# Signs of the first twelve weight pieces taken by ScalarE and multiplied in by GpSimd

## The chip, the cores and the metric

The kernel runs on one core of one Trainium2 chip. Time is device microseconds (us) for one execution. The engines are TensorE (PE; its weight loads are shown as PEld), VectorE (DVE), ScalarE (ACT), GpSimd (POOL) and SyncE (SP, which issues most of the DMAs). Each engine works through its own instructions in the order in which they stand; where it needs another engine's result it waits for a semaphore.

## The reference

A recurrent attention block (batch 4, 8 heads, 768 steps, head width 40) feeds a feed-forward block (3072 tokens, width 320, hidden width 2048):

```python
for t in range(S):
    y[:, :, t] = np.einsum('bhd,bhde->bhe', rt, state)
    Sa = np.einsum('bhde,bhe->bhd', state, at)
    state_decay = state * wt[:, :, None, :] - np.einsum('bhd,bhe->bhde', Sa, bt)
    state = state_decay + np.einsum('bhd,bhe->bhde', vt, kt)
...
h = x @ w_in
g = h * np.cos(h)
return (g @ w_out).astype(np.float32)
```

The two weight matrices `w_in` and `w_out` are given as 64-bit floats; everything else is 32-bit.

## The kernel before

**Recurrence.** The 768 steps are cut into 24 chunks of 32. Four chunks at a time share one stage that inverts small triangular matrices on VectorE, as a chain of short multiply and subtract pairs (L681 and L686 for the first four chunks, followed by the transposes L695 and L663). Each chunk then goes through short TensorE steps, named in the plan by letters: `t` (transposes of the state), `q`, `x`, `s` and `z`, with copies on ScalarE and VectorE between them (L811, L825, L850, L851, L869, the masks L875). After `z`, VectorE adds the new state and the output (L916, L925), and GpSimd multiplies both (L917 four times, L933 once, of 128x512). SyncE stores the output to a scratch tensor and reads it back, turned, as `xT`.

**Feed-forward.** Two chunks form a group of 256 tokens. For each of 12 groups TensorE multiplies `xT` by `w_in` (tile `ph`), ScalarE and VectorE form the product with the cosine, and TensorE multiplies this by `w_out` (tile `po`).

**Weights.** TensorE needs the weights as 32-bit floats, and the kernel turns the 64-bit values into these by hand, in 20 pieces of 128x512. The function is `rounded`; a piece goes through five steps, each a token in the plan with the piece's number:

- `wf`, `fetch`: SyncE loads the raw words, two 32-bit words for each value (L423).
- `wt`, `taken`: VectorE takes the mantissa's upper part (L431) and the exponent (L432) from the high word; ScalarE turns the exponent into the bits of a 32-bit power of two (Relu, L435).
- `wm`, `mantissa`: VectorE adds the low word (L444), ScalarE scales (L447).
- `wg`, `signed`: VectorE merges the high word's sign bit into the power of two (L438).
- `wp`, `product`: VectorE multiplies mantissa and signed power of two into the weight tile (L450).

The raw words lie in tiles that other stages use too (`gT` twice; `nt`, `u` and `inv` once each), the mantissa and the exponent in two buffers each. A new load into a tile waits until the last step that reads its old words is done.

**Order.** The order of all steps is written out in one string, `PLAN`; the token's place there is its place on each engine's queue that it uses. `K` and `B` tokens are filler matmuls on TensorE (tiles `busy` and `spare`), which compute nothing that is used. The pieces are worked on in the order 1, 2, 3, 0, 4, 6, 7, 9, 8, 10, 5, 11 and then 13, 12, 14 to 19. GpSimd also issues a few loads itself (L262 on POOL) and prepares operands: the copies L735, the product L741 and the copy L742, for which TensorE's transposes of `v`, `r` and `k` wait.

Of the kernel before, what the change touches and what calls it, by code (L numbers as in the profile page):

```python
# [9 lines left out]
F32 = mybir.dt.float32  # L10
I32 = mybir.dt.int32
U32 = mybir.dt.uint32
ALU = mybir.AluOpType
ACTF = mybir.ActivationFunctionType
# [114 lines left out]
def kernel(  # L129
# [43 lines left out]
    nc = tc.nc  # L173
# [55 lines left out]
    for n, fill in (("w", 1.0), ("a", 0.0), ("b", 0.0)):  # L229
        for i in range(4):  # L230
            x = slice((i - 2) * H * DP, (i - 1) * H * DP)
            if i < 2:
                t = const.tile([P, H, D if n == "b" else DP], F32, tag=f"nat_{n}{i}", name=f"nat_{n}{i}")
            else:
                t = {
                    "w": w_in_sb[:, 0, late:], "a": w_in_sb[:, 1, late:], "b": late_out
                }[n][:, x].rearrange("p (h d) -> p h d", h=H)
# [5 lines left out]
    for n in "kvr":  # L243
        t = const.tile([P, H, D], F32, tag=f"nat_{n}", name=f"nat_{n}")
# [163 lines left out]
    tick = constant(6).bitcast(BF16)[:, :1]  # L408

    WID = 512  # L410
    first_done, second_done = [], []

    def rounded(m, dst, src, by, by_sb):

        pool, tag = {"g": (sb2, "gT"), "n": (sb1, "nt"), "u": (sb1, "u"), "i": (sb1, "inv")}[WORDS[m]]
        t = {}

        def fetch():  # L420
            t["words"] = pool.tile([P, WID, 2], I32, tag=tag, name="words")
            for rows, cols, part in src:
                nc.sync.dma_start(  # L423
                    t["words"][rows, cols].rearrange("p n w -> p (n w)"), part.bitcast(I32)
                )

        def taken():
            hi = t["words"][:, :, 1]
            t["mant"] = sb2.tile([P, WID], I32, tag="mant", name="mant")
            t["expo"] = sb2.tile([P, WID], I32, tag="expo", name="expo")  # L430
            nc.vector.tensor_scalar(t["mant"], hi, 0xFFFFF, None, ALU.bitwise_and)  # L431
            nc.vector.tensor_scalar(  # L432
                t["expo"], hi, 20, 0x7FF, ALU.logical_shift_right, ALU.bitwise_and
            )
            nc.scalar.activation(t["expo"], t["expo"], ACTF.Relu, bias=to_bits, scale=2.0**23)  # L435

        def signed():
            nc.vector.scalar_tensor_tensor(  # L438
                t["expo"], t["words"][:, :, 1], -(2**31), t["expo"], ALU.bitwise_and, ALU.bitwise_or
            )  # L440

        def mantissa():
            frac = t["mant"].bitcast(F32)
            nc.vector.scalar_tensor_tensor(  # L444
                frac, t["words"][:, :, 0].bitcast(U32), 2.0**-32, t["mant"], ALU.mult, ALU.add
            )
            nc.scalar.activation(frac, frac, ACTF.Identity, bias=by_sb, scale=2.0**-20 * by)  # L447

        def product():
            nc.vector.tensor_tensor(  # L450
                dst, t["mant"].bitcast(F32), t["expo"].bitcast(F32), ALU.mult
            )

        return fetch, taken, mantissa, product, signed

    def weights():
# [5 lines left out]
        def put(dst, src, by, by_sb):  # L462
            if wide:
                work.append(rounded(len(work), dst, src, by, by_sb))
                return

            def fetch():
                for rows, cols, part in src:
                    nc.sync.dma_start(dst[rows, cols], part)

            none = lambda: None
            work.append((fetch, none, none, lambda: nc.scalar.mul(dst, dst, by), none))

        flat_out = w_out_sb.rearrange("p f n -> p (f n)")
        for j in range(NF // 4):
            cs = slice(j * WID, (j + 1) * WID)
            for i in range(2):
                put(
                    w_in_sb[:, i, cs], [(every, slice(0, WID), moe_w_in[i * P : (i + 1) * P, cs])],
                    0.5 / math.pi, by_in,  # L480
# [14 lines left out]
            first_done.append(len(work))  # L495
            for o in range(0, NF * DM, WID):
                if not 4 * j * DM <= o < 4 * (j + 1) * DM:
# [733 lines left out]
```

## Time and profile before

| What | Value |
|---|---|
| three runs, median (lowest to highest) | 762.61 us (758.38 to 766.61) |
| profiled execution | 755.39 us |
| its span, first to last instruction | 753.7 us |
| mean granted TensorE clock | 0.983 |
| busy share of PE, DVE, ACT, POOL | 93%, 71%, 53%, 33% |

The profile shows one execution. A row of the timeline gives start and duration in us, the engine, the source line, the operation, the tile that it writes and those that it reads, and how many instructions were put together; in brackets stands how long the engine had been idle and who ended that. A mean duration in a group of instructions is in ns. The chain of waits follows the work that ended last back from the end, and names at each step what released it.

The page's slices, each of 18.8 us, show the stages: until about 97 us VectorE is busy to eight or nine tenths and TensorE works on the recurrence of the first chunks; from then on TensorE is full.

```profile
PE   4659899999999999989999999999999999999995
DVE  7799888976467777568987758998367984534442
ACT  1335575775656665655645746546456444544442
POOL 8545304221241442450440442332242412321211
```

### The profile page before, as it was taken

Reading aid. Unit: us, or ns where it says so; the run is one execution under the profiler, and the core shown is the slowest. Engines: PE = TensorE matmul, PEld = TensorE weight load, DVE = VectorE, ACT = ScalarE, POOL = GpSimd, SP = SyncE. Lnnn points to the kernel's source line nnn. Section 1 sums busy time; section 2 is a strip of 40 time slices with the busy share of each in tenths; the row PEclk is TensorE's granted clock in tenths of the full one; section 3 lists DMA queues with packets and bytes.
Section 4 is the critical chain, followed back from the end, with each engine's and each line's share of the span. In section 5 each row is a group of like instructions: output and inputs, shape, how many; then the busy total and the mean of one; then the engine's idle time right before and its main releaser. Section 6 shows DMA issues by size and latency. Waiting matters only on the chain.

```text
span 753.7 us, 40220 instructions
## 1 busy us (share of the span) xinstructions
PE 702.8 (93%) x17956; PEld 578.2 (77%) x17956; DVE 534.8 (71%) x1199; ACT 398.0 (53%) x764; POOL 245.8 (33%) x427
## 2 busy tenths in 40 slices
PE   4659899999999999989999999999999999999995
PEld 2546577777777777878888888888888788888885
DVE  7799888976467777568987758998367984534442
ACT  1335575775656665655645746546456444544442
POOL 8545304221241442450440442332242412321211
PEclk9779999999999999999999999999999999999998
DMA  7667455564565657655656667557543212110000
GB/s 118 130 168 183 149 152 136 116 132 75 117 119 113 123 107 145 130 130 115 139 118 110 128 130 155 107 118 120 102 78 76 62 41 59 48 29 13 21 18 17
DMA packets 267580, 78.11 MB, mean 104 GB/s; under 512 B 229104, under 2 KB 260848, under 8 KB 267408
## 3 DMA queue, kind: packets, MB, share of 16 engines
q1 hardware_dynamic: 264976, 73.66, 46.7%
q8 instruction: 141, 2.31, 1.3%
q0 software_dynamic: 1344, 1.72, 1.2%
q10 hardware_dynamic: 1088, 0.16, 0.1%
q14 instruction: 31, 0.25, 0.1%
HBM read 54.53 MB, written 20.97 MB: 100 GB/s over the span
## 4 chain that ended last, share of the span: by engine, by line
PE 69%; DVE 13%; ACT 5%; DMA 4%; SPq 4%; issue 3%; POOL 1%; DVEq 0%; POOLq 0%; ACTq 0%
PE ph L210 28%; PE po L210 17%; PE dps L210 4%; PE x0ps L210 4%; PE gram L210 3%; PE p L210 3%; SPq L262 2%; PE sps L210 2%; PE qps L210 2%; DVE inv L659 2%; PE nps L210 2%; DVE inv_tmp L655 2%; DVE gT L1010 2%; PE sT L807 1%; DMA nat_v<-in_v_dram 1%
## 5 line engine op out<-in xcount | busy, mean ns | idle before, releaser
L210 PE MATMUL ph<-xT,w_in_sb 128*128 128x256 f32 x768 | 184.3, 386 | 2.5 <-issue 1.0
L210 PEld LDWEIGHTS ph<-xT,w_in_sb 128*128 128x128 f32 x768 | 139.8, 190 | 31.1 <-issue 12.0
L210 PE MATMUL po<-w_out_sb,gT 128*128 128x160 f32 (+1 forms) x624 | 130.3, 347 | 3.0 <-DVE gT L1010 2.3
L1002 DVE SCALAR_TENSOR_TENSOR turns<-turns,ph 128x512 f32<-128x512 f32 x96 | 63.6, 685 | 93.5 <-ACT turns L1000 93.2
L1000 ACT ACTIVATE turns<-ph,few 128x512 f32<-128x512 f32 x96 | 63.6, 686 | 120.2 <-PE ph L210 110.1
L210 PEld LDWEIGHTS po<-w_out_sb,gT 128*128 128x128 f32 x624 | 97.1, 190 | 21.5 <-DVE gT L1010 3.3
L917 POOL TENSOR_TENSOR qz<-qz,wc 128x160 f32<-128x160 f32 x92 | 40.0, 457 | 132.5 <-DVE qz L916 132.5
L1010 DVE TENSOR_TENSOR gT<-ph,turns 128x512 f32<-128x512 f32 x96 | 64.4, 684 | 21.1 <-ACT turns L1007 20.8
L1007 ACT ACTIVATE turns<-turns,few 128x512 f32<-128x512 f32 x96 | 69.3, 722 | 3.1
L1006 ACT ACTIVATE turns<-turns 128x512 f32<-128x512 f32 x96 | 60.1, 626 | 12.4 <-DVE turns L1002 12.3
L1090 POOL TENSOR_TENSOR s<-gT 128x256 f32<-128x256 f32 x36 | 26.9, 747 | 97.3 <-DVE gT L1086 97.3
L210 PE MATMUL ph<-xT,w_in_tail 64*128 64x256 f32 (+1 forms) x464 | 54.5, 396 | 0.0
L291 ACT COPY nat_a<-ws 128x416 f32<-128x416 f32 (+1 forms) x45 | 45.1, 1019 | 16.9 <-DMA wdv<-nat_a 5.7
L210 PE MATMUL po<-TW,gT 128*128 128x160 f32 x288 | 51.4, 300 | 1.8 <-DVE gT L1086 1.2
L659 DVE TENSOR_TENSOR inv<-inv,inv_tmp 128x31 f32<-128x31 f32 (+15 forms) x124 | 50.0, 404 | 4.2
L1082 POOL TENSOR_TENSOR s<-gT 128x256 f32<-128x256 f32 x36 | 27.2, 757 | 78.7 <-DVE gT L1010 72.7
L825 ACT COPY qz<-qps 40x256 f32<-40x256 f32 x92 | 33.8, 367 | 30.8 <-PE qps L210 29.3
L655 DVE TENSOR_TENSOR inv_tmp<-u,inv 128x31 f32<-128x31 f32 (+15 forms) x124 | 46.5, 375 | 2.7
L566 POOL TENSOR_TENSOR bn<-nat_b,rw 128x320 f32<-128x320 f32 x22 | 19.3, 878 | 84.8 <-DVE rw L565 39.2
L210 PEld LDWEIGHTS po<-TW,gT 128*128 128x128 f32 x288 | 42.9, 190 | 2.8 <-DVE gT L1086 1.9
L565 DVE RECIPROCAL rw<-nat_w 128x320 f32<-128x320 f32 x20 | 42.6, 2139 | 0.0
L916 DVE TENSOR_TENSOR qz<-dps,qz 128x160 f32<-128x160 f32 x92 | 29.2, 317 | 16.8 <-PE dps L210 16.8
(158 smaller groups left out, 1248.5 us busy)
## 6 DMA issues: line engine op xcount, KB each, us to landing
words<-in_moe_w_in_dram SPq DMA_DIRECT2D x8, 512.0 KB
xd<-yt SPq DMA_DIRECT2D x48, 80.0 KB
out_dram<-ot SPq DMA_DIRECT2D x24, 160.0 KB
nat_v<-in_v_dram SPq DMA_DIRECT2D x90, 40.0 KB
nat_k<-in_k_dram SPq DMA_DIRECT2D x90, 40.0 KB
nat_b<-in_b_dram SPq DMA_DIRECT2D x84, 40.0 KB
wd<-ws SPq DMA_DIRECT2D x5, 640.0 KB
nat_w<-wd SPq DMA_DIRECT2D x80, 40.0 KB
```

Of the source, the lines that this page charges most:

```text
L210: nc.tensor.matmul(o, lhsT=lhsT, rhs=rhs, start=start, stop=stop, skip_group_check=True)
L291: nc.scalar.copy(quad_part(n, q, i).rearrange("p (d t) -> p d t", t=C), ws[:, :, PARTS[i]].rearrange("p t d -> p d t"))
L565: nc.vector.reciprocal(rw, wn)
L655: nc.vector.tensor_tensor(tmp, u[:, j : j + 1, :j].to_broadcast([P, C - j, j]), x[:, j:, j : j + 1].to_broadcast([P, C - j, j]), ALU.mult,)
L659: nc.vector.tensor_tensor(x[:, j:, :j], x[:, j:, :j], tmp, ALU.subtract)
L825: nc.scalar.copy(pick(qz[rows], f * (NZ - C), (NZ, 2 * B), (1, C)), ps[f][rows, : 2 * B * C].rearrange("p (i t) -> p i t", t=C),)
L917: nc.gpsimd.tensor_tensor(z, z, wc.rearrange("p (b f m) -> p f m b" if re_laid("w", c // 4) else "p (f m b) -> p f m b", f=2, m=2)[:, :, : ...
L1000: nc.scalar.activation(t, u, ACTF.Identity, bias=rnd, scale=1.0)
L1002: nc.vector.scalar_tensor_tensor(t, t, -ROUND, u, ALU.add, ALU.subtract)
L1006: nc.scalar.activation(t, t, ACTF.Abs)
L1007: nc.scalar.activation(t, t, ACTF.Sin, bias=half_pi, scale=-2.0 * math.pi)
L1010: nc.vector.tensor_tensor(gT[:, 2 * e : 2 * e + 2, :n], phs[e], ns[e].rearrange("p (f t) -> p f t", f=2), ALU.mult)
```

## The change

For pieces 0 to 11 the step `wg` no longer runs on VectorE. Behind the Relu of `wt`, ScalarE takes the sign of the high word (seen as a 32-bit integer) and writes it back as +1.0 or -1.0 in place of the word; the step `wg`, at its old place in the plan, is a multiply of the power of two by this sign on GpSimd. Pieces 12 to 19 keep the merge on VectorE. The plan is the same.

```diff
     WID = 512
+    SIGNS = 12
...
             nc.scalar.activation(t["expo"], t["expo"], ACTF.Relu, bias=to_bits, scale=2.0**23)
+            if m < SIGNS:
+                nc.scalar.activation(hi.bitcast(F32), hi, ACTF.Sign)

         def signed():
+            if m < SIGNS:
+                power = t["expo"].bitcast(F32)
+                nc.gpsimd.tensor_tensor(power, power, t["words"][:, :, 1].bitcast(F32), ALU.mult)
+                return
             nc.vector.scalar_tensor_tensor(
                 t["expo"], t["words"][:, :, 1], -(2**31), t["expo"], ALU.bitwise_and, ALU.bitwise_or
             )
```

On GpSimd the new multiplies stand, in this order, between the loads and operands of the first three chunks: 1 and 2 before the copies L735 of chunk 2, 3 before the sums L917 and L933 of chunk 0, 0 between L933 and L741, 4, 6, 7, 9 and 8 among the following loads, 10 and 5 after the sums of chunk 1 and before the copies L735, 11 between these and the next L741.

## The prediction

> **What bounds the kernel now.** I read the page's slices first, then busy time by windows, the chain of waits in order of time, and the timeline of the stretch that the change touches. The windows (window in us, its length, then busy us and instructions of PE, PEld, DVE, ACT, POOL, then granted clock, DMA share and GB/s):
>
> ```profile
> 50.00:100.00 50.00, 43.17 (x1440) 30.70 (x1441) 45.82 (x97) 26.06 (x52) 18.04 (x26) 0.90 0.60 164
> ```
> ```profile
> 110.00:130.00 20.00, 19.30 (x429) 15.50 (x426) 16.74 (x33) 11.49 (x21) 8.36 (x16) 1.00 0.59 140
> 130.00:160.00 30.00, 28.35 (x828) 22.70 (x827) 26.62 (x53) 21.23 (x41) 9.18 (x18) 1.00 0.55 124
> ```
>
> From about 97 us on TensorE is full and its order is fixed, so whatever start it gets is carried to the end. Between 50 and 100 us the order is set by VectorE (45.8 of 50 us busy; much of the PE time there is filler), and this is where all twelve pieces are converted. The naive reading is therefore a gain: VectorE is full and the change takes twelve instructions from it. The first fence below is their group in that stretch; the chain of waits (start, us, what) says more:
>
> ```profile
> L438 DVE SCALAR_TENSOR_TENSOR expo<-words,expo 128x512 int32<-128x512 int32 x12 | 9.7, 818 | 0.2 <-ACT expo L435 0.2
> ```
> ```profile
> 67.42 0.72 ACT expo L435
> ...
> 68.83 0.51 ACT expo L435
> 69.46 1.33 ACT mant L447 x2
> ...
> 72.85 0.73 ACT expo L435
> 73.60 0.69 DVE expo L438
> ```
>
> The chain runs piece by piece through VectorE, ScalarE and back. L438 stands in it four times (52.47, 59.61, 73.60, 86.93) with 0.53+0.62+0.69+0.89 = 2.7 us. That, not 9.7, is the most that taking it away could give by this chain.
>
> **What is removed.** Twelve merges L438. One alone is 0.69 us, and 0.60 from its start to the next (80.58 to 81.18); the mean of 818 ns comes from those beside GpSimd.
>
> **What is added.** Twelve Signs on ScalarE, each right behind a Relu L435, in place on the high words (every second element, int32). No row shows one. Below lies the plain copy of 128x512 (0.59), above the re-ordering copy L291 (1.02 for 416 columns, so 1.25 for 512). I take the Relu's 0.72, the same type and size, which pushes what follows on ScalarE by 0.63 (68.83 to 69.46). Twelve multiplies of 128x512 on GpSimd. Nearest is L933, same size and engine, 1.26 to 1.72. One input fewer is L742's copy: 0.45 for 320, so 0.72 for 512, the lower end. Both inputs here lie in SBUF and one steps by two. I take 1.27, for this reason:
>
> ```profile
> 62.54 0.97 DVE L450 TENSOR_TENSOR w_out_sb<-mant,expo 128x512 f32<-128x512 f32 x1
> ...
> 62.93 1.72 POOL L933 TENSOR_TENSOR yt<-yt,wb 128x512 f32<-128x512 f32 x1
> 63.44 1.75 DVE L438 SCALAR_TENSOR_TENSOR expo<-words,expo 128x512 int32<-128x512 int32 x1
> ...
> 64.61 1.31 POOL L741 TENSOR_TENSOR kn<-nat_k,rw 128x320 f32<-128x320 f32 x1
> ...
> 65.29 1.17 DVE L450 TENSOR_TENSOR w_in_sb<-mant,expo 128x512 f32<-128x512 f32 x1
> 65.86 0.90 POOL L742 COPY vvm<-nat_v 128x320 f32<-128x320 f32 x1
> ```
> ```profile
> 117.39 1.26 POOL L933 TENSOR_TENSOR yt<-yt,wb 128x512 f32<-128x512 f32 x1
> ```
>
> Alone L933 takes 1.26 and L438 0.69. Together they take 1.72 and 1.75, and each ends about one lone duration after the other did: 63.51 + 1.2 = 64.7, + 0.6 = 65.2, + 0.8 = 65.9, + 0.6 = 66.5. They take turns. So a multiply costs VectorE its 1.27 us wherever VectorE has two-input SBUF work of its own, and this work replaces 0.60 us.
>
> The Trainium skill says the same as a rule (SBUF — State Buffer, "SBUF: two separate sides"): VectorE and GpSimd share one pair of ports under an exclusive lock, held for the whole instruction. These rows agree. By that rule the sum is the one below; without it, it is the first rival's.
>
> **The wait it adds.** The product L450 on VectorE now waits for the multiply, and the multiply for Sign and for its place on GpSimd's queue. From the end of Relu to the product: Sign 0.63, hand-over 0.08 (VectorE to GpSimd at 61.15 to 61.23), multiply 1.27, hand-over 0.03, in all 2.0 us. Before, these rows left (Relu's end to product, by piece): 1: 16.0, 2: 0.8, 3: 4.1, 0: 5.5, 6: 1.3, 4: 3.3, 7: 1.0, 9: 2.7, 8: 10.4, 10: 9.0, 11: 1.1, 5: 5.2. Four are under 2.0. Behind a waiting product stand on VectorE the next piece's two extractions, the copies L851 and masks L875 and L789 for which TensorE's recurrence waits, and the running sums L916.
>
> ```profile
> 72.85 0.72 ACT L435 ACTIVATE expo<-expo,few 128x512 int32<-128x512 int32 x1
> ...
> 73.51 0.72 ACT L447 ACTIVATE mant<-mant,few 128x512 f32<-128x512 f32 x1
> 73.60 0.69 DVE L438 SCALAR_TENSOR_TENSOR expo<-words,expo 128x512 int32<-128x512 int32 x1 [0.19 <-ACT expo L435]
> ...
> 74.58 0.68 DVE L450 TENSOR_TENSOR w_in_sb<-mant,expo 128x512 f32<-128x512 f32 x1
> ```
>
> **The sum, in the order of time.** Each step is the delay of the recurrence against before.
>
> 1. Up to 61 us, piece 1. On GpSimd its multiply stands behind four load issues (43.96 to 46.3), so it runs at 46.3 to 47.6, inside the chained inversion on VectorE (46.1 to 48.8, no idle, two SBUF inputs). It holds that up by its 1.27, about 1.2, up to the transpose L663 for which TensorE waits (52.61). The saved merge at 52.32 lies behind that. Piece 2's longer way makes the mask L875 late by 1.8, ending at 58.85; TensorE wants it at 59.95 and is itself 1.2 late: hidden. **+1.2.**
> 2. 61 to 66.4, pieces 3 and 0. GpSimd's order is multiply 3, the sums L917, L933, multiply 0, L741, L742. Multiply 3 lies before the sums and before the product L450 at 62.54, both free. Multiply 0 takes the turn that merge 0 had: 1.27 for 0.60. **+0.7.**
> 3. To 70.8, pieces 4 and 6. The chain is ScalarE: Relu, copies, Relu, then L447 twice, product 6 at 70.82. Two Signs come in (+1.26) and multiply 6 then needs 1.27: Relu 6 ends 69.57 + 1.26 + 0.08 + 1.27 + 0.03 = 72.2. **+1.4.**
> 4. Piece 7, the fence above: 73.57 + 2.0 = 75.6 for 74.58. **+1.0.**
> 5. Pieces 9 and 8. Two Signs push the copy L869 from 77.27 to 78.5; multiply 8 (78.7 to 80.0) then holds L444, which starts near 80.0 instead of 77.8; L447 ends 81.35, product 9 at 81.4 for 79.36. The two saved merges lie behind. **+2.0.**
> 6. 85 to 97, pieces 10, 5, 11. GpSimd's queue is in order: multiplies 10 and 5 stand ahead of the copies L735, multiply 11 ahead of L741. L741 ended at 91.4 and its transpose ran at 95.53. Now multiply 5 waits for Relu and Sign 5 (to 92.1, done 93.4), the copies end 94.3, multiply 11 95.6, L741 96.4. **+1.0.**
>
> Sum +7.3 us. From piece 12 on the code is as before, TensorE is the bound, and I see nothing that takes the delay back. On SyncE's queue, fetches now wait for the multiply instead of the merge, with loads of w, stores of yt and the read of xT behind them. The fetch at 55.61 is used at 66.39, so its 2 us are covered; the others move with the steps above.
>
> The profiled execution: 753.7 span + 1.7 around it = 755.4 us; with the sum, 762.7. The three runs have a median of 762.6, 7.2 above the profiled one, so I put the same sum on that: 769.9, say **770**.
>
> **Rivals.**
> *Multiplies beside VectorE.* If they did not take turns, step 1 goes, step 2 goes to 0, step 5 falls to the two Signs (1.3), step 6 to 0.3: +4.0, 766.6. Against it: the rows at 62 to 66. For it: none, except that VectorE's own work has gaps. 0.11.
> *The cover holds, not slower.* Eight of twelve products leave more than 2.0 us. If the ones under it are also hidden by other waits (VectorE already waits 0.61 and 1.56 us for TensorE before L916), the chain loses what L438 has in it: 0 to −2.7, so 760 to 762.6. It decides once multiplies end before the product's place in the queue at pieces 2, 6, 7, 11. Against it: at 6 and 7 the chain of waits goes right through this loop. 0.12.
> *Heavier multiplies.* At the 1.72 of the contended row, or with a price for the stepping input, some eight multiplies in the steps cost 0.45 more: +10.9, 773.5. A lower granted clock would add too: it is 0.50 where TensorE idles, at 50 to 58 us. 0.17.
> *Not what it says.* Sign might need its own function table. The trace has one ACT_TABLE_LOAD, 1.28 us; 24 of them would give +31 (793). The changed program has one as well. 0.01. The Trainium skill (ScalarE: Activation LUTs, "What ACT_TABLE_LOAD costs") has about 2.66 us a switch, the drain included, by which it would be an estimated +64 us.
>
> **Chances and range.** Forecast 0.59. One per cent is 7.6 us, about what a measurement of this kernel can tell from no change, and the sum lies almost on it. What is not in the sum (hand-overs, clock) only adds, so a little over half of the forecast (0.33) goes beyond, with the heavier case and the table: slower 0.51. Within: 0.26 of the forecast, 0.11, and most of the cover (0.08): 0.45. Faster by over 1% asks for more than the chain holds: 0.04. Range: from the edge of the cover (763) to the heavier case (773.5), with half the spread of the three runs (4) and a Sign at its upper end in the four chain steps (4 x 0.5) on top: 780.
>
> **What would show it.** Right: L438's successors on GpSimd near 1.3 to 1.7 us; products L450 waiting for GpSimd at pieces 6, 7, 9; inversion rows near 46 us stretched by about 1.2; the first real ph matmul at 104 instead of 96.8, and the rest shifted by as much. Wrong: that matmul before 99, products that do not wait, multiplies and VectorE rows overlapping at their lone durations, or a shift that shrinks after 110 us.

## The result, and the profile after

Over 20 runs of each kernel the changed kernel took a median of 766.66 us (763.59 to 773.14), the kernel before 761.55 us (756.38 to 766.61). The ratio is 1.008, with a 95% interval of 1.0061 to 1.01: slower by about 6.1 us of 761.6, and by less than one per cent. The two medians differ by 5.1 us; the ratio is not formed from them.

The profiled execution of the changed kernel took 766.23 us (span 764.5), near its median. The profiled execution of before (755.39) lies below all of its 20 timed runs, so the difference of the two profiles, 10.8 us, is more than the change costs. For that reason I use a second profile of each kernel as well, called "again" below: spans of 756.3 for before and 766.2 for after.

The stretch from 50 to 100 us by windows (start and end, length, then busy us and instructions of PE, PEld, DVE, ACT and POOL, the granted clock, the DMA share and GB/s), in the profile after:

```profile
50.00:100.00 50.00, 39.53 (x1305) 26.57 (x1306) 34.48 (x78) 26.25 (x54) 26.76 (x31) 0.76 0.52 135
```

VectorE, which was busy for 45.82 of these 50 us, is busy for 34.48, and the stretch is slower: 97 instructions had been done on VectorE by its end, now 78. VectorE was relieved and waits. For whom, is in the list of waits of the profile after between 50 and 110 us (who waited, for what: us in all, times, longest):

```profile
POOL expo L443 <- ACT words L438: 18.7, 8, 7.6
...
DVE w_in_sb L457 <- POOL expo L443: 8.4, 4, 2.7
```

In the changed file L443 is the multiply, L438 the Sign, L457 the product (L450 before), L451 the addition of the low word (L444 before); L688, L693 and L670 are the inversion (L681, L686, L663 before). The group of the multiplies (count, then shortest, median and longest in ns, and from where to where), and two products on VectorE that wait for them:

```profile
L443 POOL TENSOR_TENSOR expo<-expo,words x12: 1282/1298/1572, 46.3 to 104.0; 128x512 f32<-128x512 f32 x12
```
```profile
76.44 0.69 DVE L457 TENSOR_TENSOR w_in_sb<-mant,expo 128x512 f32<-128x512 f32 x1 [2.70 <-POOL expo L443]
...
81.20 0.69 DVE L457 TENSOR_TENSOR w_in_sb<-mant,expo 128x512 f32<-128x512 f32 x1 [1.72 <-POOL expo L443]
```

These are pieces 6 and 7. Before, product 7 stood at 74.58 right behind other work of VectorE. In the chain of waits of the profile after, the multiply stands four times with more than a microsecond, as L438 stood there four times before, though only piece 10 is among both: L438 stood at pieces 1, 3, 7 and 10, the multiply stands at 0, 4, 10 and 11 (start, us, what):

```profile
68.08 1.28 POOL expo L443
...
73.12 1.58 POOL expo L443
...
97.69 1.42 POOL expo L443
...
103.98 1.29 POOL expo L443
```

L438 had 2.7 us in its four rows; these four are 5.6 us.

### The profile page after: what moved, and what is told of

The parts are those of the page before. It is cut to its first block, busy times and chain, and to the rows that moved or that the text cites. A ratio compares the mean times of both kernels' runs of the same rounds, so it can differ in the third digit from the quotient of the medians.

```text
span 764.5 us, 40262 instructions
## 1 busy us (share of the span) xinstructions
PE 707.9 (93%) x17956; PEld 581.2 (76%) x17956; DVE 533.7 (70%) x1187; ACT 404.4 (53%) x776; POOL 260.9 (34%) x439
## 3 DMA queue, kind: packets, MB, share of 16 engines
q0 software_dynamic: 1344, 1.72, 1.2%
## 4 chain that ended last, share of the span: by engine, by line
PE 69%; DVE 13%; ACT 5%; issue 4%; SPq 4%; DMA 2%; POOL 1%; DVEq 0%; POOLq 0%; ACTq 0%
PE ph L210 27%; PE po L210 18%; PE dps L210 4%; PE x0ps L210 4%; PE p L210 3%; PE gram L210 3%; SPq L262 3%; PE sps L210 2%; PE qps L210 2%; DVE inv L666 2%; DVE inv_tmp L662 2%; DVE gT L1017 2%; PE nps L210 2%; PE sT L814 1%; DVE turns L1009 1%
```

## The experiments

Every kernel was timed beside the kernel before. Medians and ratios are over the timed runs; marks such as "the first ph" are read from the one profile of each kernel and scatter by a us or two.

| Kernel | median us | before beside it | ratio (95%) | worked out, us |
|---|---|---|---|---|
| before, again | 762.62 | 761.58 | 1.001 (0.9986 to 1.0034) | +0.8 |
| neither Sign, multiply nor merge | 760.15 | 761.58 | 0.9991 (0.996 to 1.0023) | -0.7 |
| Signs alone | 762.58 | 761.58 | 1.0018 (0.9995 to 1.0041) | +1.4 |
| multiplies alone | 767.49 | 761.58 | 1.0077 (1.0047 to 1.0107) | +5.9 |
| piece 1 only | 763.92 | 761.40 | 1.0023 (0.9993 to 1.0053) | +1.8 |
| all but piece 1 | 765.05 | 761.40 | 1.0058 (1.0025 to 1.0091) | +4.4 |
| multiplies of 64 columns | 763.79 | 761.40 | 1.0034 (1.0006 to 1.0061) | +2.6 |
| before, with unawaited multiplies | 772.62 | 761.40 | 1.0145 (1.0107 to 1.0184) | +11.0 |
| after, again | 767.10 | 761.82 | 1.0072 (1.0046 to 1.0098) | +5.5 |
| multiply 1 ahead of the load issues | 766.89 | 761.82 | 1.0068 (1.0038 to 1.0098) | +5.2 |
| pieces 2, 6, 7, 11 only | 762.55 | 761.82 | 1.0013 (0.9979 to 1.0046) | +1.0 |
| pieces 0, 3, 5, 8, 10 only | 763.02 | 761.82 | 1.0009 (0.9977 to 1.004) | +0.7 |

The last column is the ratio's distance from 1 times the median beside it.

**Before, again**: the unchanged file, to learn the spread of a profile.

> The kernel before, unchanged, run and profiled again. The profiled execution before was 755.4 us, the lowest but one... of its kind: the runs of the same kernel lie between 756.4 and 766.6, and the profile of after (766.2) lies in the middle of its own runs (763.6 to 773.1). If the two profiles compared so far were unequal draws, this profile's span is nearer to 760 than to 753.7, and the steps where it is later (start of the first sums L916, before at 60.8 us; first product of piece 6, at 70.8) show where a run's luck lies. If the profile of before is typical, its span is again 752 to 756 and the 10.8 us between the profiles are the change's. Times: ratio 1.000.

Its span was 756.3 and its timed median 762.62. The profile reaches the first ph matmul at 98.02 us, where the first one had 96.76, so two profiles of one kernel differ there by 1.3 us. Its 758.06 us is the lowest of its twelve runs, and the first lay below all of its twenty, so both profiles of before show short executions; those of after do not.

**What the merges were worth.** For pieces 0 to 11 the merge is gone and nothing stands in its place. The sign of these weights is left out of what is computed.

```diff
-            if m < SIGNS:
-                nc.scalar.activation(hi.bitcast(F32), hi, ACTF.Sign)
...
             if m < SIGNS:
-                power = t["expo"].bitcast(F32)
-                nc.gpsimd.tensor_tensor(power, power, t["words"][:, :, 1].bitcast(F32), ALU.mult)
                 return
```

> For pieces 0 to 11 the sign is left out: no merge on VectorE, no Sign, no multiply (those weights come out positive). It prices what taking the merge away can give. The chain of waits held 2.7 us of it: -1 to -2.7 us. By the naive reading (VectorE bound, 12 x 0.60) -7 us.

Taking twelve merges away for nothing gives 0.7 us, with an interval from 3.0 faster to 1.8 slower. The windows of this kernel:

```profile
50.00:100.00 50.00, 42.01 (x1435) 29.49 (x1436) 39.75 (x87) 26.64 (x53) 17.65 (x26) 0.90 0.59 160
```

VectorE does 6 us less than before in these 50 us and the first ph comes at 97.80, between the two profiles of before. The naive gain of some 7 us is refuted: VectorE was busy, but little of what waited for its merges could start earlier. A kernel that replaces the merges by other work should not gain more than this one, which does nothing in their place.

**The halves.** With the Signs alone the multiply is left out, and with the multiplies alone the Sign, so that the power of two is multiplied by the raw high word. Both compute other values than the reference.

```diff
# Signs alone
             if m < SIGNS:
-                power = t["expo"].bitcast(F32)
-                nc.gpsimd.tensor_tensor(power, power, t["words"][:, :, 1].bitcast(F32), ALU.mult)
                 return
```
```diff
# multiplies alone
-            if m < SIGNS:
-                nc.scalar.activation(hi.bitcast(F32), hi, ACTF.Sign)
```

> For pieces 0 to 11 the Sign on ScalarE stays, the multiply is left out (those weights come out positive). By the steps on record the Signs push L447 before product 6 (+1.2), product 7 (+0.3) and the copies L869 (+1.2), and the missing merges give back about 1: +1 to +2.5 us. If ScalarE's share costs nothing, as with 'neither': -1 to -2.7.

> For pieces 0 to 11 the multiply on GpSimd stays and takes the raw high word instead of its sign (those weights come out wrong); no Sign on ScalarE. By the steps on record, taking turns: piece 1 inside the inversion +1.2 (the profile of after shows 2.4), turn of multiply 0 +0.7, product 6 +0.1, product 7 +0.4, multiply 8 before L444 +0.9, the last pieces +0.4: +3.7 to +5 us. If multiplies ran beside VectorE: +0.5 at most.

The Signs alone cost 1.4 us, an interval that holds zero; the multiplies alone cost 5.9, as much as the whole change (5.5 and 6.1). By the end times the price of the change is that of the multiplies, and the Signs add nothing measurable on top; in the profiles the first ph comes at 99.0 with the Signs alone, at 103.1 with the multiplies alone and at 104.8 and 106.6 with both.

**Turns, or a longer way?** Two kernels separate the cost of holding VectorE from that of waiting. The first is the kernel before, merges and all, with twelve multiplies of 128x512 on GpSimd at the places of `wg` that nobody waits for; they read the identity and write a tile that later work overwrites.

```diff
         def signed():
+            if m < SIGNS:
+                four = pick(ident, 0, (0, 4), (1, P))
+                to = TW.rearrange("p j i f n -> p (j i f n)")[:, :WID].rearrange("p (a n) -> p a n", n=P)
+                nc.gpsimd.tensor_tensor(to, four, four, ALU.mult)
             nc.vector.scalar_tensor_tensor(
```

> As before, merges on VectorE and all, and in addition, at the place of each of the twelve merges in the plan, GpSimd multiplies 128x512 of tiles that nobody waits for (two constant inputs in SBUF, a result that is not used). No wait is added for any other engine. If VectorE and GpSimd take turns: twelve times 1.27 = 15 us of turns, less what falls into VectorE's idle time and into stretches where it is not what bounds: +7 to +13 us. If they run side by side: 0 to +1 (GpSimd's own queue a little later).

It is 11 us slower, 0.9 us for each multiply, though none is waited for. (These are pure additions; in the change the merges go.) If VectorE and GpSimd worked side by side, the cost could only be that of GpSimd's own queue, and VectorE's own rows would keep their durations. They do not. These are the windows from 30 us to the first ph, of before and of this kernel:

```profile
30.00:96.76 66.76, 53.50 (x1910) 37.45 (x1909) 61.31 (x139) 32.65 (x69) 32.94 (x52) 0.86 0.57 150
```
```profile
30.00:108.29 78.29, 55.72 (x1912) 39.38 (x1911) 71.95 (x138) 33.13 (x69) 47.43 (x64) 0.83 0.50 128
```

VectorE is given no work more (138 instructions for 139) and is busy 71.95 us for 61.31, and the first ph comes 11.5 us later: the cost lies in VectorE's rows. The timeline, with the multiply at L442, shows the turns:

```profile
66.82 1.75 DVE L443 SCALAR_TENSOR_TENSOR expo<-words,expo 128x512 int32<-128x512 int32 x1
...
68.67 1.34 DVE L455 TENSOR_TENSOR w_in_sb<-mant,expo 128x512 f32<-128x512 f32 x1
```
```profile
66.31 1.72 POOL L938 TENSOR_TENSOR yt<-yt,wb 128x512 f32<-128x512 f32 x1
67.98 1.48 POOL L442 TENSOR_TENSOR TW<-ident 128x512 f32<-128x512 f32 x1
```

The merge, 0.69 alone, takes 1.75 and ends at 68.57, 0.54 behind the sum L938 (68.03). The multiply, 1.05 where nothing disturbs it, takes 1.48 and ends at 69.46; the product, 0.69 alone, ends at 70.01, 0.55 behind it. Each ends about one lone duration after the one that it met. This agrees with the rule that the prediction drew on (the Trainium skill, SBUF — State Buffer, "SBUF: two separate sides"): the pair of ports is held by one engine at a time.

The second keeps every instruction, wait and queue place of the change and makes the multiplies short, 64 of 512 columns. The sign of the other columns is left out.

```diff
-                nc.gpsimd.tensor_tensor(power, power, t["words"][:, :, 1].bitcast(F32), ALU.mult)
+                nc.gpsimd.tensor_tensor(power[:, :64], power[:, :64], t["words"][:, :64, 1].bitcast(F32), ALU.mult)
```

> As after, Signs whole, but the multiply takes the first 64 of 512 columns only (the others keep a positive sign). Every wait and every place in a queue is as in after; the multiply's length, and with it its hold on the ports, falls from 1.3 to some 0.2 to 0.4 us. If the length is the price (turns, and the loop's 1.27): as with the Signs alone, +1 to +3 us. If the added wait and GpSimd's queue order are the price: still near +6.

It costs 2.6 us of the change's 5.5 to 6.1. First the product 0 of the profile after, then this kernel's multiply 0 on GpSimd and the product behind it on VectorE:

```profile
69.40 1.33 DVE L457 TENSOR_TENSOR w_in_sb<-mant,expo 128x512 f32<-128x512 f32 x1 [2.40 <-POOL expo L443]
```
```profile
65.99 0.32 POOL L443 TENSOR_TENSOR expo<-expo,words 128x64 f32<-128x64 f32 x1
```
```profile
66.35 1.34 DVE L457 TENSOR_TENSOR w_in_sb<-mant,expo 128x512 f32<-128x512 f32 x1 [1.44 <-POOL expo L443]
```

The product waits 1.44 here, against 2.40 in the profile after: the multiply is 0.96 shorter and the wait is 0.96 shorter. So about half of the price is the length of the multiplies, in turns taken and in the waits that they lengthen, and the rest, of which the Signs alone measured 1.4, is the longer way through ScalarE and GpSimd whatever the multiply's length. The interval of this kernel, 0.5 to 4.6 us, makes it a rough share, and 2.6 also lies in the range that the expectation gave for the length as the whole price.

**Piece 1, and the rest.** The test of step 1 against the others.

```diff
-    SIGNS = 12
+    SIGNS = (1,)        # or (0, 2, 3, 4, 5, 6, 7, 8, 9, 10, 11)
...
-            if m < SIGNS:
+            if m in SIGNS:
```

> The change for piece 1 alone (the other eleven keep the merge). Step 1 on record: its multiply falls into the inversion on VectorE and holds it up by 1.2 us; the profile of after shows one pair of the inversion stretched from 0.28 to 2.36 us and the transpose L663/L670 2.4 us later. By the steps +1 to +2.5 us. If the inversion has slack behind it: 0 or -0.6. In the profile the stretched subtract near 45.4 us is to be seen again.

> The change for eleven pieces, all but piece 1. By the steps on record +7.3 - 1.2 = +6.1; by what was measured of the whole (+6.1) less piece 1's 1 to 2.5: +3.5 to +5. If piece 1 were all of it: 0.

Piece 1 alone costs 1.8 (from -0.5 to +4.0), the other eleven 4.4 (from 1.9 to 6.9); together 6.2, which agrees with the whole change. The first interval holds zero, so the end times agree with the split and do not show it. The marks do not add up: with piece 1 alone the first ph comes at 103.83, with the other eleven at 102.72, 6.4 and 5.3 us behind the mean of the two profiles of before, where the whole change is 8.3 behind it. What makes piece 1 alone late there is taken up, in part, below. The held inversion row shows with piece 1 alone as with all twelve (DVE L693 at 45.43, 2.34 us); with the other eleven alone the inversion has its old length.

**Where multiply 1 stands.** The next kernel moves only `wg` of piece 1 in the plan, from behind GpSimd's load issues to ahead of them.

```diff
- ... in:1 v:1 L:2:v:p:r ... wf:2 wg:1 wp:1 ...
+ ... in:1 v:1 wg:1 L:2:v:p:r ... wf:2 wp:1 ...
```

> As after, but the multiply of piece 1 stands earlier on GpSimd's queue: behind the copies L742 (to 44.0 us) and ahead of the six load issues, not behind four of them. The steps on VectorE are in the same order. In after, one inversion pair there was held from 45.4 to 47.6, some 0.9 us longer than the multiply's own row (46.3 to 47.6). If the hold begins while GpSimd is still issuing the loads ahead of the multiply: now one pair near 44 us is held by 1.0 to 1.4 us in all, and the transpose ends near 54.0 instead of 54.9 (52.5 to 52.7 before). If the multiply holds VectorE by 2.1 us wherever it stands: 54.9 again. In time -0.5 to -1 us against after, within the scatter.

At 766.89 it is as slow as the change. But the inversion, from the start of its first transpose to the end of the transpose `rt`, takes 17.2 us, where the two profiles after have 18.65 and 18.02 and those before some 16.5. First the row of VectorE and the load issues beside it before the change, then the multiply and VectorE's held row of the profile after, then those of the moved kernel:

```profile
45.00 0.28 DVE L686 TENSOR_TENSOR inv<-inv,inv_tmp 128x120 f32<-128x120 f32 x1
```
```profile
45.13 2.30 POOL L262 DMA_DIRECT2D nat_r<-in_r_dram  x4
```
```profile
46.26 1.30 POOL L443 TENSOR_TENSOR expo<-expo,words 128x512 f32<-128x512 f32 x1
```
```profile
45.35 2.36 DVE L693 TENSOR_TENSOR inv<-inv,inv_tmp 128x120 f32<-128x120 f32 x1
```
```profile
43.30 1.28 POOL L443 TENSOR_TENSOR expo<-expo,words 128x512 f32<-128x512 f32 x1
```
```profile
42.94 0.47 DVE L788 TENSOR_TENSOR ag<-gram,su 128x128 f32<-128x128 f32 x2
43.34 0.50 DVE L796 TENSOR_TENSOR vvm<-gram,su 128x128 f32<-128x128 f32 x2
43.76 0.97 DVE L688 TENSOR_TENSOR inv_tmp<-u,inv 128x126 f32<-128x126 f32 x1
```

In the profile after, VectorE's row of 0.28 is held for 2.1 us more, and it stands still before the multiply's row begins: alone it would have ended at 45.63, and the multiply starts at 46.26. In the moved kernel the first part of the multiply lies beside two rows that read TensorE's output (`gram`), which keep their durations (0.47 and 0.50, as before), and only the next row is held, by 0.7. So the place was worth 0.8 to 1.5 us at the inversion, but the end did not follow: the first ph came at 103.87, 0.95 before that of the second profile after.

**Tight and loose products.** By the prediction, pieces 2, 6, 7 and 11 lack the room for the longer way, and pieces 0, 3, 5, 8 and 10 have it. The edit is again the tuple: `SIGNS = (2, 6, 7, 11)` and `SIGNS = (0, 3, 5, 8, 10)`.

> The change for pieces 2, 6, 7 and 11 alone, the four whose product stood less than 2.0 us behind the Relu. By the steps on record, product 6 late by 0.8 (one Sign ahead of it, not two), 7 by 1.0, 11 by 0.5, piece 2 hidden: +2 to +3 us. If only such pieces cost anything (the wait loop alone), it is nearly all of not1: +4.

> The change for pieces 0, 3, 5, 8 and 10 alone, whose products stood 4.1 us or more behind the Relu, so that the wait is covered. By the turns at the ports multiply 0 costs 0.7, 8 about 1 (it stands before L444), 10 and 5 about 0.7 together: +2 to +3 us. If the price is the wait alone: 0 or below (the merges given back).

+1.0 (from -1.6 to +3.5) and +0.7 (from -1.8 to +3.0). The intervals hold zero as well as the +2 to +3 that was expected of each, so the end times of these two decide nothing: the parts of the change are smaller than what a dozen runs can tell. In their profiles the first ph comes at 101.18 and 100.91, 3.8 and 3.5 us behind the mean of before, but both profiled executions (766.36 and 764.89 us) were among the longer of their twelve.

**After, again**: the changed kernel unchanged, for a second profile and a second measurement.

> The changed kernel, unchanged, profiled and timed again beside the runs of this job: ratio near 1.008. Its profile tells what of the 10.8 us between the first two profiles belongs to the change: by the sum of steps and the ratio the first real ph matmul is some 6 to 9 us later than in the two profiles of before (96.8 and 98.0), and the stretch from there to the end is of the same length (656.9 and 658.3 before) within its own scatter of a few us.

+5.5 us, in agreement with the first +6.1.

## Why the prediction was right, and where a size was off

The sign and the mechanism were right: slower, because multiplies on GpSimd take turns with VectorE's work and because the product waits for a longer loop through ScalarE and GpSimd, while the merges that go away are nearly worthless. The sum of +7.3 stands against +6.1 and +5.5. The forecast of 770 lies 3.3 above the median of 766.7; 1.1 of this is the base, 762.6 over three runs against 761.55 over twenty. The larger chance, 0.51, had been put on more than one per cent slower, and the measured 0.8 lies under that.

Step by step, as distances between marks in the two profiles of before and the two of after:

| Step | from, to | before | after | measured | predicted |
|---|---|---|---|---|---|
| 1 | first transpose of the inversion to its end | 16.38, 16.60 | 18.65, 18.02 | +1.4 to +2.3 | +1.2 |
| – | to the first running sum | 8.36, 8.34 | 9.44, 9.52 | +1.1 to +1.2 | nothing |
| 2 | first running sum to the extraction behind product 0 | 5.57, 5.58 | 6.36, 6.36 | +0.8 | +0.7 |
| 3 | to product 6 | 4.43, 4.43 | 5.78, 5.76 | +1.3 | +1.4 |
| 4 | to product 7 | 3.76, 3.74 | 4.76, 4.78 | +1.0 | +1.0 |
| 5 | to product 9 | 4.78, 5.26 | 6.76, 6.75 | +1.5 to +2.0 | +2.0 |
| 6 | to the first ph | 17.40, 17.95 | 18.67, 18.32 | +0.4 to +1.3 | +1.0 |

Steps 2 to 5 came out within 0.1 us, or within the difference of the two profiles of before.

For steps 4 and 5 these lengths are not proof by themselves. In the kernel with piece 1 alone, where pieces 6 to 9 keep their merges, the same two stretches take 4.80 and 6.75, as long as in the profiles after. There TensorE is what comes late: its `qps` run took 0.81 before, where the granted clock was 1.00 from 65 to 75 us, and takes 1.29 here, where it was 0.67 from 70 to 75 us. ScalarE's copies wait for that run, and the Relu of piece 7 stands behind these copies; in step 5 the mask waits 1.69 for TensorE's `sps` run. First the run, then the merge of piece 7 (L445 here), which waits for that Relu:

```profile
73.00 1.29 PE L210 MATMUL qps<-rT,s 40*40 40x32 f32 x64
```
```profile
77.14 0.69 DVE L445 SCALAR_TENSOR_TENSOR expo<-words,expo 128x512 int32<-128x512 int32 x1 [1.15 <-ACT expo L436]
```

In the profile after the waits are those of the prediction: product 7 waits 1.72 for its multiply, and in step 5 the mask waits for ScalarE's copy, which follows the two Signs, and the addition of the low word is held beside the multiplies of 9 and 8.

```profile
85.29 0.29 DVE L882 TENSOR_TENSOR x<-sps,su 128x128 f32<-128x128 f32 x1 [1.79 <-ACT x L876]
85.50 1.60 DVE L451 SCALAR_TENSOR_TENSOR mant<-words,mant 128x512 f32<-128x512 uint32 x1
```

So it is these rows that bear the steps out. Equal lengths from two different waits are a coincidence as far as the runs show.

*Step 6* went the way that was described in the main, and its +1.0 was helped by luck: two terms that it left out lie on opposite sides. Multiply 11 has to wait for its own Sign; by the rows of before this is done at 95.6, and the step let the multiply end then. In the profile after the multiply waits 0.77 for it behind the copies. On the other side, before, TensorE's transpose of `k` did not wait, and ph then waited 0.60 us for `xT`. After, the transpose waits for L748 (L741 before), which stands behind multiply 11, and ph follows without a wait:

```profile
103.98 1.28 POOL L443 TENSOR_TENSOR expo<-expo,words 128x512 f32<-128x512 f32 x1 [0.77 <-ACT words L438]
```
```profile
106.13 0.66 PE L528 MATMUL kT<-ident,kn 128*128 128x128 f32 x4 [1.67 <-POOL kn L748]
106.63 1.68 PE L210 MATMUL ph<-xT,w_in_sb 128*128 128x256 f32 x7
```

So the transfer's 0.60 covered a part of the 1.67.

*Step 1 is the term that was mis-sized.* It held that multiply 1 "holds that up by its 1.27, about 1.2". The hold is there, at the row that was named, but it is 2.1 us in that row and 1.4 to 2.3 over the inversion, since VectorE is held before the multiply's row begins. Behind the inversion stands a term that the sum put at nothing: TensorE adds a wait put down to "issue", before its third run of `below` matmuls: 0.49 and 0.28 in the profiles of before, 1.32 and 1.57 in those after. With it the first running sum comes 1.1 us later behind the inversion's end. The other half of step 1 stood: the mask of piece 2's chunk ends at 60.14, and TensorE, late itself, wants it at 63.4, so piece 2's longer loop is hidden.

By the profiles the whole delay at the first ph is 8.3 us (105.7 on average for after, 97.4 for before), more than the sum; by the timed runs it is 5.5 to 6.1 at the end, less than the sum. From the first ph to the end, before took 656.9 and 658.3, after 657.9 and 661.4, and the ten other kernels, the same code there but for the shift, 659.0 to 665.9. That scatter is larger than what is to be found. Whether some 2 us are given back behind 97 us, or the profiled executions were late draws at that mark, stays open; the prediction's "nothing that takes the delay back" was neither shown nor refuted.

*The turns* go further than the prediction had it, which counted them for VectorE's work with two inputs. In the profile after two extractions with one input (L433, before L432; their median is 0.42) are held as well: one takes 1.50 beside the multiply of piece 10, one takes 1.52 beside that of piece 5, which starts at 100.85.

```profile
100.98 1.52 DVE L433 TENSOR_SCALAR expo<-words 128x512 int32<-128x512 int32 x1
```

*The rivals.* The time does not tell the forecast from the first rival: its 766.6 is the measured median to 0.1 us, which is chance, and its +4.0 lies just below the first interval (4.6 to 7.6) and inside the second (3.5 to 7.5). That VectorE and GpSimd work side by side is refuted by the unawaited multiplies (+11) and their rows. That the cover holds is refuted by the waits of 2.70 and 1.72 at products 6 and 7, and by the interval of the result; its upper bound was sound, as the kernel without merges shows (-0.7, in its span of 0 to -2.7). Heavier multiplies: the median is 1298 ns and the longest 1572, so the 1.27 was right and the 1.72 wrong. The lower granted clock came, 0.76 and 0.78 between 50 and 100 us against 0.90, and the steps that I followed are no longer than their sums without it; but with piece 1 alone a low clock goes with the same lengths, so how much of the change's time is the clock stays open. A function table was not loaded again.

## What to carry to other kernels

A busy engine is not a bound: taking twelve instructions from VectorE was worth what they hold in the chain of waits, at most 2.7 us, and measured as 0.7. Before work is moved to GpSimd, add its whole duration to VectorE wherever rows like these show that the two take turns, because 1.3 us of turn replaced 0.6 us here; and add the new loop to each step's slack before the consumer, one piece at a time. When several small terms are wanted apart, measure them at marks inside the profile and not at the end, where two profiles of one kernel differ by more than the terms; and read at each mark which wait made the length, because another wait can make the same one.

## What was not expected of the hardware

VectorE is held before the other engine's row begins. In the profile after, by at least 0.63 us (a row of 0.28 that started at 45.35 and did not end, the multiply at 46.26); in the second profile by at least 0.2 (45.04 with 0.27, the multiply at 45.54). In both, GpSimd is in its row of load issues at that moment and the multiply stands next. Where the multiply was released by ScalarE instead, as at 100.85, no such early hold is seen: the extraction at 100.64 keeps its 0.43 and the multiply takes 1.37. Load issues with no multiply among them hold nothing: before, VectorE's rows keep their lengths beside the four from 45.13 to 47.43. With the multiplies of 64 columns at the same place the hold is 0.3 us in all (rows of 0.41 and 0.44 for 0.28 and 0.27), and in the kernel with unawaited multiplies a second row is held behind the multiply's end (47.95, 1.07 for 0.28). The profile calls its spans on GpSimd rough, so a row that is drawn late is another reading. The cause stays open; the moved kernel can't tell, since VectorE read TensorE's output when its multiply began.

TensorE's "issue" wait before the third `below` is 1.1 to 1.8 us in all eight profiles without the merge of piece 1 (the kernel with neither among them), and 0.2 to 0.5 in five of the six with it; the kernel with all but piece 1 has 1.84 and breaks the rule. It looks tied to what VectorE does at that moment, but no run takes it apart.
